# V tiles of a decode-attention kernel loaded on a second DMA queue

## The chip, the cores and the metric

The kernel runs on one core of a Trainium2 chip. The metric is the device time of one execution in microseconds, the median of several runs. The engines are TensorE (PE), VectorE (DVE), ScalarE (ACT), GpSimd (POOL) and SyncE (SP). Loads from HBM to the on-chip memory are done by the core's 16 DMA engines; an engine's instruction queue issues them, and each issuing engine has a DMA queue of its own (SyncE's is q1 in the profile).

## What is computed

One decode step (one token for each of 4 batches) of a transformer block: attention over the last 4096 positions of a cache, then a gated MLP. Cut to what matters:

```python
# x [4,1,576]; k_cache, v_cache [4, 16, 16384, 128]; 32 query heads on 16 KV heads; all bf16
W = 4096
q = (layernorm(x) @ wq)                       # 32 heads of 128
k = k_cache[:, :, Sk - W:, :]                 # 64 MiB are read of it
v = v_cache[:, :, Sk - W:, :]                 # and 64 MiB of it
p = softmax(q . k * 128**-0.5)
h = x + (p @ v) @ wo
hn = layernorm(h)
out = h + (relu(hn @ W_gate) * (hn @ W_up)) @ W_down     # F = 4608
```

## The kernel before

The cache windows are cut into 16 K tiles and 16 V tiles of 4 MiB. Tile g holds four KV heads of batch g // 4, as 128 partitions of 32 KiB. Four slots of the on-chip array `arena` take them in turn (`ring_slot`, `NSLOT = 4`). W_q uses one of the slots first. From K4 and V0 on the order is K4, V0, K5, V1, and so on to K15, V11, then V12 to V15; from K6 and V2 on, K tiles alternate between slots 0 and 2 and V tiles between slots 1 and 3.

The program is written as one list of operations for each engine, with named dependencies (`Prog`). Each engine takes its list in order and waits by semaphore for what an operation depends on. `place` (L216) adds a load: it finds in `owner` who reads the 64-element blocks that it will overwrite, makes the load depend on that reader (`("QK", g)` or `("PV", g)`), and puts it on SyncE's list. `add_kv` (L235) does that for a K or V tile; its load is issued at L242. All loads but that of x (L337, ScalarE's queue) are on SyncE's list, in the order: W_q (L251, L255), the tiles, W_o (L266), the weights of the MLP (L269 to L278), W_down in five parts (L284).

What uses the tiles, for each g from 0 to 15:

- VectorE transposes K tile g in place (`turn_k`, L424), in one instruction or, for g = 4, 8 and 12, in two halves.
- TensorE then does QK g (`pe_qk`, L448 and the helper line L34): 32 matmuls. When it ends, the slot of K tile g is free.
- At the end of a batch (g = 3, 7, 11, 15) comes the softmax: row maximum, exponential, transpose (`soft`, L453 to L470), and `remap` (L475 on TensorE, L482 on ScalarE and L487 on VectorE), which lays out the probabilities for PV. For batch 0 it stands between the two halves of the transpose of K tile 4.
- From g = 4 on TensorE does PV g - 4 after QK g (`pe_pv`, L509 and L34): 32 matmuls that read V tile g - 4. When it ends, that slot is free.
- `select_o` (L519 to L526, on ScalarE and VectorE) takes the result of PV out of PSUM.

After QK15 follow, on TensorE's list: PV11, `remap` of the last batch, PV12 to PV15, the output projection (L617), the second layernorm, the gate and up projections (GU, L666), and W_down's (L690), which reads HHT, the hidden values transposed by VectorE at L679. GpSimd's list holds only memsets and selects that set up constants (L289 to L331).

Of the kernel before, what the change touches and what calls it, by code (L numbers as in the profile page):

```python
# [20 lines left out]
NTILE = B * KVH // 4  # L21
# [4 lines left out]
TILE = 16384  # L26
# [94 lines left out]
def bass_sequential_preLN__sliding_block_cached__glu_gated_reglu__decode_kernel(  # L121
# [12 lines left out]
    with ExitStack() as es:  # L134
        cnt = [0]

        def sb(name, shape, dt):
            return es.enter_context(nc.sbuf_tensor("sb_" + name, shape, dt))

        P = Prog()  # L140
# [8 lines left out]
        arena = sb("arena", [128, AW], BF16)  # L149
# [63 lines left out]
        land = {}  # L213
        uses = {}

        def place(name, off, size, reader, make, key=None):  # L216
            deps = []
            for blk in range(off // 64, (off + size) // 64):
                r = owner.get(blk)
                if r is not None and r not in deps:  # L220
                    deps.append(r)
                owner[blk] = reader
            semk = key or "d_" + "_".join(str(v) for v in name)
            P.dma("sync", ("L",) + name, make, semk, deps)
            land[name] = off

        ring = [(-1 - 2 * NTILE) % NSLOT]
# [1 line left out]
        def ring_slot():  # L229
            s = ring[0] % NSLOT  # L230
            ring[0] += 1
            return s


        def add_kv(kind, g):  # L235
            b, qd = divmod(g, 4)
            s = ring_slot()
            off = slot0 + s * TILE
            cache = A_k_cache if kind == "K" else A_v_cache
            src = cache[b, 4 * qd:4 * qd + 4, SK - WIN:SK, :].rearrange("a (p t) d -> p a (t d)", p=32)  # L240
            place((kind, g), off, TILE, ("QK", g) if kind == "K" else ("PV", g),
                  lambda e: e.dma_start(out=arena[:, off:off + TILE], in_=src), key=f"slot{s}")  # L242


        def main_rows(W):
# [2 lines left out]
        def last_rows(W):  # L248
# [3 lines left out]
        s = ring_slot()  # L252
        wq_off = slot0 + s * TILE
        place(("wq", 0), wq_off, TILE, "QMM",
              lambda e: e.dma_start(out=arena[:, wq_off:wq_off + TILE], in_=main_rows(A_wq)), key=f"slot{s}")  # L255
        for g in range(NTILE):
            add_kv("K", g)
            if g >= 4:
                add_kv("V", g - 4)
# [3 lines left out]
        for g in range(NTILE - 4, NTILE):  # L263
            add_kv("V", g)
        place(("wo",), WO_OFF, H * D, "WO",
              lambda e: e.dma_start(out=arena[:, WO_OFF:WO_OFF + H * D], in_=A_wo.rearrange("(p r) n -> p (r n)", p=128)))  # L266
        gu_off = {}
        off = WO_OFF + H * D
        place(("gu", 0, 4), off, F, ("GU", 1, 4), lambda e, off=off: e.dma_start(  # L269
            out=bass.AP(tensor=arena, offset=off, ap=[[2 * AW, 64], [1, F]]), in_=B_W_gate[512:576, :]))  # L270
        P.dma("sync", ("L", "gu", 1, 4), lambda e, off=off: e.dma_start(
            out=bass.AP(tensor=arena, offset=AW + off, ap=[[2 * AW, 64], [1, F]]), in_=B_W_up[512:576, :]), "d_gu_1_4")
# [9 lines left out]
        for r0, r1 in zip(WD_ROWS, WD_ROWS[1:]):  # L282
            place(("wd", r0), wd_off + r0 * D, (r1 - r0) * D, ("DOWN", 1),
                  lambda e, r0=r0, r1=r1: e.dma_start(  # L284
                      out=arena[:, wd_off + r0 * D:wd_off + r1 * D],
                      in_=B_W_down.rearrange("(p r) n -> p (r n)", p=128)[:, r0 * D:r1 * D]))
# [18 lines left out]
                                                in_=c_qm[:, :, :].rearrange("p q (h j) -> p q h j", j=4),  # L305
# [4 lines left out]
                                                in_=to_v[:, :, :].rearrange("p n (k a) -> p n k a", a=4),  # L310
# [14 lines left out]
        for sg in range(2):  # L325
            pool(f"c_toq{sg + 1}", lambda e, sg=sg: e.affine_select(
                out=toq[:, :, :, :], in_=toq[:, :, :, :],
                pattern=[[0, 16], [32 * (1 - 2 * sg), 4], [0, 2]], compare_op=ALU.is_ge, fill=0.0, base=31 * (1 - sg), channel_multiplier=2 * sg - 1),
                [f"c_toq{sg}"])
        pool("c_oT", lambda e: e.memset(oT[:, :, :], 0.0))  # L330
        pool("c_hnT", lambda e: e.memset(hnT[:, :, :], 0.0))  # L331
        dve("c_m4", lambda e: e.tensor_reduce(out=m4[:, :], in_=c_m4[:, :, :], axis=AX.X, op=ALU.max), ["c_m41"])
        dve("c_par0", lambda e: e.tensor_tensor(out=par[:, 0:1], in0=m4[:, 0:1], in1=m4[:, 2:3], op=ALU.add), ["c_m4"])
        dve("c_par", lambda e: e.tensor_scalar(out=par[:, 1:2], in0=par[:, 0:1], scalar1=-1.0, scalar2=1.0,
# [206 lines left out]
        def finish_o():  # L541
            for q in range(4):
                for qd in range(4):
# [17 lines left out]
                                              in_=bass.AP(tensor=e8, offset=0, ap=[[8, 128], [0, 4], [1, 8]])), ["c_e8", "c_selc0"])  # L561
# [47 lines left out]
        for a in range(8):  # L609
            for n in range(2):  # L610
                for j in range(4):
# [4 lines left out]
                    else:  # L616
# [6 lines left out]
                                             in_=bass.AP(tensor=psb, offset=512 + 224, ap=[[4096, 128], [1, 64], [0, 2]])), ["part1"])  # L623
# [27 lines left out]
        for g in range(2):  # L651
            for c in (4, 0, 1, 2, 3):
                part_ = c if c == 4 or (c == 3 and g) else 0
                for m in range(3):
                    for j in range(4):
                        first = m == 0 and j == 0 and (c in (0, 4) or part_ == 3)
                        deps = [("L", "gu", g, part_)] if first else []
# [20 lines left out]
        for i in range(2):  # L678
            dve(("HHT", i), lambda e, i=i: e.transpose(  # L679
                out=hhT[:, 576 * i:576 * i + 576].rearrange("p (r q) -> p r q", q=32),  # L680
                in_=bass.AP(tensor=pp, offset=3712 + 18 * i, ap=[[PPW, 128], [1, 18], [36, 32]])), [("HH", m) for m in range(3)])
# [14 lines left out]
        for r in range(36):  # L696
# [3 lines left out]
            for n in range(2):  # L700
                deps = []
# [39 lines left out]
```

## Time and profile before

| | |
|---|---|
| median of 3 runs | 378.30 us (378.28 to 378.32) |
| the profiled execution | 378.22 us |
| its span in the profile | 377.0 us |
| busy: TensorE, VectorE, ScalarE, GpSimd | 213.8, 228.8, 53.7, 10.5 us |
| bytes moved, mean rate | 159.74 MB, 424 GB/s |
| SyncE's queue: share of the 16 DMA engines' span | 98.7% |
| issue to landing, median: K tiles, V tiles | 26.3, 28.5 us |
| mean granted clock of TensorE | 0.796 of full speed |

Busy time is the time in which an engine executes. The share of a DMA queue is the time that its packets took, over 16 times the span. "Issue to landing" is the time from the DMA instruction to the arrival of its last byte, so it contains the wait behind earlier transfers. The lines of the chain "that ended last" follow back, from the last instruction, what released each step.

### The profile page before, as it was taken

To read this page: it belongs to the slowest core of one execution; us is meant where nothing else is said; L and a number is where in the kernel's file an instruction comes from. 1 tells how busy PE (TensorE), PEld (TensorE's weight loads), DVE (VectorE), ACT (ScalarE), POOL (GpSimd) and SP (SyncE) were. 2 spreads that over 40 slices of the span, in tenths; PEclk is the share of its full clock that TensorE was granted. 3 is DMA by queue.
4 is the path that set the end of the run, shared out by engine and by line. 5 is a ranking of instruction groups with operands and counts; after the bars stand their busy time and mean duration, and the time that the engine had idled before them with its cause. 6 is when DMAs were issued, how large, how long until landed. Compare 5 with 4: busy or idle time off the path is not lost.

```text
span 377.0 us, 2556 instructions
## 1 busy us (share of the span) xinstructions
PE 213.8 (57%) x1462; PEld 39.9 (11%) x694; DVE 228.8 (61%) x164; ACT 53.7 (14%) x84; POOL 10.5 (3%) x29
## 2 busy tenths in 40 slices
PE   0404443239919091749282844664655787886658
PEld 0000000001001010001010100110000101002316
DVE  4088878779292969584847778665749433333240
ACT  3093000211000114010101140101010411112010
POOL 8200000000000000000000000000000000000000
PEclk9966666659969788696877786989695968998686
DMA  8999999999999999999999999999999999999996
GB/s 334 445 445 428 405 445 442 396 442 445 398 435 445 442 433 403 442 445 435 407 436 445 435 414 431 441 438 431 417 442 438 426 417 442 418 433 437 427 414 256
DMA packets 6378, 159.74 MB, mean 424 GB/s; under 512 B 728, under 2 KB 864, under 8 KB 1248
## 3 DMA queue, kind: packets, MB, share of 16 engines
q1 hardware_dynamic: 6360, 159.59, 98.7%
q8 instruction: 8, 0.13, 0.1%
q14 instruction: 2, 0.02, 0.0%
q10 hardware_dynamic: 8, 0.00, 0.0%
HBM read 159.58 MB, written 0.00 MB: 423 GB/s over the span
## 4 chain that ended last, share of the span: by engine, by line
DMA 60%; PE 20%; DVE 18%; SPq 1%; issue 0%; ACT 0%
DMA sb_arena<-in_A_k_cache_dram 53%; DVE sb_arena L424 16%; PE psb L34 11%; DMA sb_arena<-in_B_W_down_dram 7%; PE psb L448 4%; PE psb L509 3%; PE psb L690 2%; DVE sb_o_tmp L522 1%; DVE sb_pp L487 1%; SPq L242 0%; PE psb L475 0%; SPq L255 0%; ACT sb_out_sb L709 0%; SPq L251 0%; DVE sb_f L534 0%
## 5 line engine op out<-in xcount | busy, mean ns | idle before, releaser
L424 DVE STREAM_TRANSPOSE sb_arena<-sb_arena 128x8192 f32<-128x8192 f32 (+1 forms) x19 | 139.9, 7366 | 67.3 <-DMA sb_arena<-in_A_k_cache_dram 67.3
L448 PE MATMUL psb<-sb_arena 128*32 128x512 bf16 x256 | 42.8, 633 | 119.6 <-DVE sb_arena L424 119.5
L34 PE MATMUL psb<-sb_arena,sb_pp 128*128 128x512 bf16 (+1 forms) x386 | 108.7, 392 | 0.0
L509 PE MATMUL psb<-sb_arena,sb_pp 128*128 128x512 bf16 x128 | 50.8, 397 | 8.9 <-DVE sb_o_tmp L522 8.9
L519 ACT COPY sb_o_tmp<-psb 32x512 f32<-32x512 f32 x32 | 18.5, 577 | 182.0 <-PE psb L34 181.7
L34 PE MATMUL psb<-sb_arena 128*32 128x512 bf16 x256 | 43.6, 642 | 0.0
L522 DVE TENSOR_TENSOR sb_o_tmp<-psb,sb_fm 32x512 f32<-32x512 f32 x32 | 21.7, 678 | 18.6 <-PE psb L34 18.1
L448 PEld LDWEIGHTS psb<-sb_arena 128*32 128x32 bf16 x256 | 9.5, 119 | 161.9 <-DVE sb_arena L424 132.7
L509 PEld LDWEIGHTS psb<-sb_arena,sb_pp 128*128 128x128 bf16 x128 | 12.8, 100 | 116.6 <-issue 116.6
L526 DVE TENSOR_REDUCE sb_o_sel<-sb_o_tmp 128x128 f32<-128x512 f32 x16 | 17.7, 1106 | 0.5
L467 ACT ACTIVATE sb_pp<-psb,sb_hx 128x1024 bf16<-128x1024 f32 x4 | 4.5, 1113 | 79.4 <-DVE sb_hx L464 79.4
L487 DVE TENSOR_TENSOR sb_pp<-psb,sb_m 128x1024 bf16<-128x1024 f32 x8 | 9.3, 1206 | 4.9 <-PE psb L475 4.9
L482 ACT ACTIVATE sb_pp<-psb,sb_m 128x512 bf16<-128x512 f32 x16 | 9.7, 690 | 14.9 <-PE psb L475 14.9
L525 DVE TENSOR_TENSOR sb_o_tmp<-sb_o_tmp,sb_fm 64x512 f32<-64x512 f32 x16 | 11.0, 689 | 0.5
L415 ACT COPY sb_arena<-sb_q_keep 32x256 bf16<-32x256 bf16 x8 | 9.7, 1451 | 0.1
L690 PE MATMUL psb<-sb_arena,sb_pp 128*32 128x272 bf16 (+1 forms) x70 | 7.6, 396 | 3.7 <-DMA sb_arena<-in_B_W_down_dram 3.7
L401 DVE CAST sb_pp<-psb 128x512 bf16<-128x512 f32 x1 | 2.4, 2427 | 10.5 <-PE psb L381 10.5
L470 DVE STREAM_TRANSPOSE sb_pp<-sb_pp 128x1024 bf16<-128x1024 bf16 x4 | 5.0, 1245 | 5.1 <-ACT sb_pp L467 5.1
L475 PE MATMUL psb<-sb_pp,sb_to_v 128*32 128x256 bf16 x64 | 4.3, 400 | 6.3 <-DVE sb_pp L470 6.3
L690 PEld LDWEIGHTS psb<-sb_arena,sb_pp 128*32 128x32 bf16 x70 | 6.0, 131 | 5.1 <-DMA sb_arena<-in_B_W_down_dram 3.9
L34 PE MATMUL psb<-sb_arena,sb_hnT 128*32 128x384 bf16 x80 | 6.5, 407 | 0.0
L381 PE MATMUL psb<-sb_arena,sb_xnT 128*32 128x512 bf16 x16 | 2.6, 628 | 6.3 <-DMA sb_arena<-in_A_wq_dram 6.3
(120 smaller groups left out, 81.5 us busy)
## 6 DMA issues: line engine op xcount, KB each, us to landing
sb_arena<-in_A_k_cache_dram SPq DMA_DIRECT2D x16, 4096.0 KB, 26.3
sb_arena<-in_A_v_cache_dram SPq DMA_DIRECT2D x16, 4096.0 KB, 28.5
sb_arena<-in_A_wo_dram SPq DMA_DIRECT2D x1, 4608.0 KB, 24.8
sb_arena<-in_B_W_gate_dram SPq DMA_DIRECT2D x1, 4608.0 KB, 27.7
sb_arena<-in_A_wq_dram SPq DMA_DIRECT2D x1, 4096.0 KB, 12.7
sb_arena<-in_B_W_up_dram SPq DMA_DIRECT2D x1, 3456.0 KB, 27.3
sb_arena<-in_B_W_down_dram SPq DMA_DIRECT2D x1, 2160.0 KB, 26.5
sb_arena<-in_B_W_down_dram SPq DMA_DIRECT2D x1, 1440.0 KB, 29.6
```

Source lines behind the costliest of these rows:

```text
L34: return e.add_instruction(mybir.InstMatmult(name=e.bass.get_next_instruction_name(), engine=mybir.EngineType.PE, ins=[e.lower_ap(rhs), e. ...
L415: act("QW", lambda e, i=i, q=q: e.copy(out=bass.AP(tensor=arena, offset=32 * i * AW + 2 * i + q, ap=[[AW, 32], [512, 16], [136, 4], [32, 4]]),
L424: dve(("TRA", g), lambda e: e.transpose(out=dst, in_=src), [("L", "K", g)] if lo == 0 else [])
L448: fn = lambda e, out_=out_, lhsT=lhsT, rhs=rhs, start=start, stop=stop: e.matmul(out_, lhsT=lhsT, rhs=rhs, start=start, stop=stop, skip_gr ...
L482: act(("EV", b, 0), lambda e, a=a: e.activation(out=bass.AP(tensor=pp, offset=2 * a, ap=[[PPW, 128], [8, 2], [32, 128], [1, 2]]), in_=bank ...
L487: dve(("EV", b, 1), lambda e, n=n: e.tensor_tensor(out=bass.AP(tensor=pp, offset=16 + 8 * n, ap=[[PPW, 128], [32, 128], [2, 4], [1, 2]]), ...
L509: fn = lambda e, lhsT=lhsT, rhs=rhs, k=k, j=j: e.matmul(bank[2 + j], lhsT=lhsT, rhs=rhs, start=(k == 0), stop=(k == 7), skip_group_check=True)
L519: act(("OSC", g), lambda e, j=j: e.copy(out=o_tmp[32 * j:32 * j + 32, 0:512], in_=bank[2 + j][32 * j:32 * j + 32, :]), [("PV", g), ("OSEL" ...
L522: dve(("OSD", g), lambda e, j=j: e.tensor_tensor(out=ot(32 * j, 32), in0=bank[2 + j][32 * j:32 * j + 32, :].rearrange("p (t d) -> p t d", ...
L525: dve(("OS", g), lambda e: e.tensor_tensor(out=ot(64, 64), in0=ot(64, 64), in1=fmb(64, 64), op=ALU.mult), [("OSC", g)])
L526: dve(("OSEL", g), lambda e: e.tensor_reduce(out=o_sel[:, qd, b, :], in_=o_tmp[:, 0:512].rearrange("p (t d) -> p d t", d=DH), axis=AX.X, o ...
L690: return lambda e: e.matmul(out_, lhsT=lhsT, rhs=w[:, lo:hi], start=start, stop=stop, skip_group_check=True)
```

## The change

`place` takes the issuing engine as an argument. For V tiles 0 to 11 the load goes on GpSimd's list instead of SyncE's; these loads are collected in `side` and appended after GpSimd's last memset. Their dependencies, slots and destinations are the same as before. Each of them has a semaphore of its own instead of its slot's. K tiles, V tiles 12 to 15 and all weights stay on SyncE's list, in the same order.

```diff
-        def place(name, off, size, reader, make, key=None):
+        def place(name, off, size, reader, make, key=None, eng="sync"):
...
             semk = key or "d_" + "_".join(str(v) for v in name)
-            P.dma("sync", ("L",) + name, make, semk, deps)
+            if eng == "sync":
+                P.dma(eng, ("L",) + name, make, semk, deps)
+            else:
+                side.append(lambda: P.dma(eng, ("L",) + name, make, semk, deps))
             land[name] = off
...
+        side = []
...
             place((kind, g), off, TILE, ("QK", g) if kind == "K" else ("PV", g),
-                  lambda e: e.dma_start(out=arena[:, off:off + TILE], in_=src), key=f"slot{s}")
+                  lambda e: e.dma_start(out=arena[:, off:off + TILE], in_=src), key=None if kind == "V" and g < NTILE - 4 else f"slot{s}",
+                  eng="gpsimd" if kind == "V" and g < NTILE - 4 else "sync")
...
         pool("c_hnT", lambda e: e.memset(hnT[:, :, :], 0.0))
+        for make in side:
+            make()
```

## The prediction

> **What bounds the kernel now.** I read the page's table of queues first, then the waits of SyncE's own queue and its timeline, then the landing of single transfers, and last the chain that ended last, from 252 us on.
>
> ```profile
> span 377.0 us, 2556 instructions
> q1 hardware_dynamic: 6360, 159.59, 98.7%
> L424 DVE STREAM_TRANSPOSE sb_arena<-sb_arena 128x8192 f32<-128x8192 f32 (+1 forms) x19 | 139.9, 7366 | 67.3 <-DMA sb_arena<-in_A_k_cache_dram 67.3
> ```
>
> One queue, SyncE's, moves 159.59 MB and keeps the 16 DMA engines 98.7% busy. The transposes on VectorE (8.71 us a K tile) wait 67.3 us in all for K. The timeline gives the pace: the transposes of K6 and K15 start on landing, at 103.20 and 278.16 us, so a pair of 4 MiB tiles takes 174.96 / 9 = 19.44 us: 9.72 us a tile, 431.5 GB/s.
>
> ```profile
> 46.13 0.54 SPq L242 DMA_DIRECT2D sb_arena<-in_A_v_cache_dram  x1
> 55.87 0.54 SPq L242 DMA_DIRECT2D sb_arena<-in_A_k_cache_dram  x1
> 66.97 0.53 SPq L242 DMA_DIRECT2D sb_arena<-in_A_v_cache_dram  x1
> 85.00 0.54 SPq L242 DMA_DIRECT2D sb_arena<-in_A_k_cache_dram  x1
> 92.01 0.54 SPq L242 DMA_DIRECT2D sb_arena<-in_A_v_cache_dram  x1
> ```
>
> These are V0, K5, V1, K6 and V2, each issued when its slot came free (after QK1, QK2, QK3, QK4 and PV0). V0 and V1 landed 27.6 and 26.2 us after issue, at 73.7 and 93.2. K3, K4 and K5 landed at 54.30, 64.02 and 83.46 (starts of their transposes), in the order of issue. Here is the queue's thinnest place: at 85.00, when K6 is issued, only V1 is left ahead, for 8.2 us more.
>
> ```profile
> 252.02 26.12 DMA sb_arena<-in_A_k_cache_dram
> 278.16 8.72 DVE sb_arena L424
> 290.74 0.58 PE psb L509
> 340.90 26.55 DMA sb_arena<-in_B_W_down_dram
> 367.49 7.54 PE psb L690 x66
> ```
>
> K15 lands at 278.14, is transposed, QK15 ends and PV11 starts at 290.74. From there TensorE, VectorE and ScalarE run a serial tail (softmax of the last batch, PV12 to PV15, the projections). The chain switches to W_down's transfer at 340.90, but the tail is almost as late: the first half of HHT is ready at about 365.6, 1.9 us before W_down's first part at 367.45; the last GU matmuls also waited some 0.4 us for W_up. So two paths end within 2.3 us of each other: all the bytes, and "PV11 starts, then the tail".
>
> **What the change moves.** No byte, no compute instruction and no slot. V0 to V11 leave SyncE's queue (12 issues of 0.54 us, none on the path) for GpSimd's, behind the last memset there, which ends at 12.2 us. Nothing is queued behind them on GpSimd, so their waits hold up nobody else; each has a semaphore of its own, which costs nothing that a row shows. Each tile still waits for the reader of its slot. K5, K6 and the rest no longer stand behind a V issue, but in the timeline they never did: each left as soon as its own QK ended. So the unblocking is worth 0.
>
> What does change is the order of delivery, if GpSimd's V tile shares the engines with K tiles issued before it. The trace of before has no two bulk queues at once. Its nearest row is x, issued on ScalarE's queue at 0.93 us, after W_q's 512 KB on SyncE's at 0.80; x was in use at 3.16 while the 512 KB landed at 4.0: another queue does not wait for the backlog. Ends for V's share are therefore nothing until K's queue is empty, and everything; I take half, since both tiles come in the same 128 rows of 32 KiB. In the Trainium skill, "DMA: Bandwidth & Descriptors", section "Queues, rings and completion order", says that each DMA engine serves its queues in turn, packet by packet; x's row agrees, and no run shows it for bulk.
>
> A transfer's fixed part: 512 KB took 3.2 us to land, 1.2 of it at 431.5 GB/s, so 2.0; I put 1.3 ahead of the data and 0.7 behind. An issue on GpSimd has no row; the ends are 0 and 3.5 us more than SyncE's (its longest row, the memset of L298), and I take 1.0, near its selects and larger memsets (0.95 for L330).
>
> Step 1: K4 loses its place. V0's data start beside K3's at about 47.4. K3's last 6.2 us take 12.4, landing at 60.5. V0 ends at 66.8. K4 ends when all three have, in V0's old place: 73.7 instead of 64.02, 9.7 later. QK3 ends at 60.5 + 8.7 + 3.9 = 73.1, and V1 is issued then; K5 and V1 share, and both are in by 93.2, where V1 was before.
>
> Step 2: the engines run dry. From K4's landing to QK4's end it is 85.0 - 64.0 = 21.0 us (half a transpose, the softmax of batch 0, the other half, QK4). QK4 now ends at 94.7, so K6 is issued at 94.7 and not at 85.0. The data of K5 and V1 are through at about 92.4; K6's start at 96.0. That is 3.6 us with nothing to move, where the queue was never empty. All bytes end 3.6 us later.
>
> Step 3: phase. PV0 runs 94.7 to 101.6, so V2's data start at 101.6 + 1.0 + 1.3 = 103.9, when K6 has 1.8 of its 9.7 us left. At half speed K6 ends at 107.5. K7, issued at 105.5 after QK5, follows until 126.9; V2 ends at 123.3. From there each queue has its next tile in time (K8 is issued near 121, V3 near 112.5), and both deliver one tile each 19.44 us. K15 ends at 126.9 + 8 x 19.44 = 282.4 and lands at 283.1 (before 278.14). V11 ends at 123.3 + 9 x 19.44 = 298.3 and lands at 299.0 (before 259.03 + 28.8 = 287.8). V11 is later by more than 3.6 because V12, on SyncE's queue behind K15, takes half the engines from 282.4 on, where before it came after V11.
>
> Step 4: the tail. QK15 would end at 283.1 + 8.7 + 3.9 = 295.7; V11 at 299.0 is last. PV11 starts 8.3 us later than 290.74, and the tail with it. The covers of 1.9 and 0.4 us are used up: 8.3 - 2.3 = 6.0. The bytes, 3.6 late, are now hidden behind it. The profiled execution took 378.22 us (span 377.0 and 1.2 around it; the median is 378.30): 378.22 + 6.0 = **384.2 us**.
>
> Bounds. With GpSimd's issue at 0, V2 lands 1.0 earlier and the sum is 383.2; at 3.5 it is about 386. The rate with both queues has the ends 423 GB/s (the page's mean over the span) and 444 (the answer for 24 to 44 us); over the 250 us from 46 to 298 that is +5.0 or -7.0 us. I keep 431.5, the row for the same tiles.
>
> **Rivals.**
>
> Uneven shares or another phase. All bytes up to K15 and V11 are through by 287.8 + 3.6 = 291.4, and V12 adds as much as V11 has left at K15's end. If both land together, QK15 ends at 291.4 + 12.6 = 304.0 and PV11 is 13.3 late: 389.2. If V11 is a whole tile behind, it lands at 301.1, 10.4 late: 386.3. The least is 7.0 late, when both waits end at once (382.9). With V starved outright, V12 to V14 could pass V11, three tiles or 29 us more: up to some 405. For this: nothing fixes the share. Against: equal rows. Chance 0.25 in all. The Trainium skill, "SBUF — State Buffer", section "SBUF: two separate sides" (its box on DMAs issued from GpSimd), speaks against the change: GpSimd cannot write its descriptors while VectorE holds their shared port in a two-port mode. The rows against its applying here: L424 does 8192 elements in 8.71 us, 0.94 a ns, and the other VectorE rows of the loop are no faster; if V's issues waited for L424 all the same, V would fall behind K, up to the 386.3 above.
>
> Nothing moves: V tiles are delivered in the order of issue after all, or V0's start is so late that K4 keeps its place. Then K6 leaves at 85.0 and everything stays: 378.3. For: 98.7% is already full. Against: x's row. Chance 0.08. The Trainium skill, "DMA: Bandwidth & Descriptors", section "Issuing engines are not separate DMA queues", says that the engine chosen only saves its issue time; taken alone that is this case, for 0.54 us an issue is off the path.
>
> Faster: two queues side by side move 444 GB/s instead of 431.5. From 46 to 298 us that takes back 7.0 of the tail's 8.3 and, with the covers, 6.0 - 7.0 = -1.0: 377.2. It decides from about 443 GB/s on. For: the answer for 24 to 44 us. Against: tile after tile, landings at 9.72 us over 175 us with the queue full. Chance 0.07.
>
> **How the numbers follow.** The forecast has 0.60 (382.9 to 386.3 with the cost of GpSimd's issue, 379 to 389 with the rate). A difference of 0.2%, 0.76 us, is about what a measurement of this kernel can tell. Faster: the third rival and a sliver of the forecast at the best rate, 0.08. Same: the second rival, 0.08. Slower: the rest, 0.84. The range goes from 378.0, which takes in "nothing moves", to 391.0, which takes in the tiles landing together with a slightly lower rate; left out are the faster case and a starved queue.
>
> **What would show it.** In the changed profile: 48 MiB on a queue of GpSimd's; K4's transpose starting near 73.7 instead of 64.02; K6 issued near 94.7 and a dip in the GB/s row just after 92 us, worth 3.6 us; K landings 19.44 us apart from K7 on; V11 landing near 299 and as what PV11 waits for; W_down no longer the last wait, with L690 waiting for VectorE's HHT. Wrong, if K4 lands at 64, if the pair's pace with both queues is far from 19.44 us, or if W_down's transfer still ends the chain.

## The result, and the profile after

The changed kernel takes 383.65 us (median of 4 runs, 383.32 to 384.02), the kernel before beside it 378.31 us: the ratio is 1.0141, 95% interval 1.0124 to 1.0159. It is 5.3 us slower. The profiled execution took 383.58 us (span 382.3).

Line numbers after differ from those before: V and K tiles are issued at L247, K's transpose is L432, PV is L517, HHT is L687, W_down's matmuls are L698, W_down is loaded at L290.

The page of the changed kernel, the DMA rows of its 40 slices (9.6 us each) and its queues (packets, MB, share of 16 engines):

```profile
DMA  8999999995999999999999999999999999999996
GB/s 330 439 439 439 434 401 425 439 439 223 384 437 439 440 435 434 415 425 425 439 439 437 435 432 418 425 428 435 439 439 432 427 425 422 456 417 447 400 421 259
q1 hardware_dynamic: 4632, 109.26, 66.8%
q0 software_dynamic: 1728, 50.33, 30.6%
```

q0 is GpSimd's queue, with the twelve V tiles. The tenth slice stands out: 223 GB/s and half busy, where the kernel before had no such slice. The stretch from 89 to 100 us, before and then after. The columns are the stretch, its length, the busy time of TensorE, of its weight loads, of VectorE, ScalarE and GpSimd (in brackets the number of instructions), TensorE's granted clock, the DMA share and GB/s:

```profile
89.00:100.00 11.00, 10.86 (x66) 1.80 (x26) 6.68 (x7) 1.16 (x2) 0.00 (x0) 1.00 1.00 427
```

```profile
89.00:100.00 11.00, 9.11 (x57) 1.42 (x23) 9.81 (x2) 0.00 (x0) 0.00 (x0) 0.80 0.58 232
```

The packet records of the trace place the gap: 15 of the 16 DMA engines end their last packet of K5 and V1 at 91.3 to 91.7 us (one straggler at 92.72), and the first packets of K6 start at 96.22 to 97.0 us. K6's issue, with K7's in the same row (before, K6 was issued at 85.00):

```profile
94.90 11.39 SPq L247 DMA_DIRECT2D sb_arena<-in_A_k_cache_dram  x2
```

The chain that ended last, changed kernel (start, us, what):

```profile
36.49 37.29 DMA sb_arena<-in_A_k_cache_dram
73.81 4.45 DVE sb_arena L432
...
105.75 23.40 DMA sb_arena<-in_A_k_cache_dram
129.18 8.72 DVE sb_arena L432
...
263.31 26.17 DMA sb_arena<-in_A_k_cache_dram
289.51 8.72 DVE sb_arena L432
...
302.14 0.32 PE psb L517
...
351.75 26.94 DMA sb_arena<-in_B_W_down_dram
378.74 1.63 PE psb L698 x20
```

The first line is K4: 37.29 us from issue to landing, at 73.79 instead of 64.00. Its transpose, the softmax of batch 0 and QK4 follow, and K6 is issued at 94.90 instead of 85.00. K15 lands at 289.49 (before 278.14), PV11 starts at 302.14 (before 290.74), and the end is again a part of W_down. All landings of W_down are 5.4 us later than before: its first part at 372.85 (367.45), its last at 380.12 (374.72).

Summed from the packets, the bytes moved fall behind those of the kernel before by 2.30 MB up to 105 us, 5.3 us at 431.5 GB/s, and are 2.29 MB behind at 340 us: all of it is lost in that one gap, and nothing more in the 190 us with two queues that follow.

### The profile page after: what moved, and what is told of

It is laid out like the page before. It is cut to its first block, busy times and chain, and to the rows that moved or that the text cites. A ratio compares the mean times of both kernels' runs of the same rounds, so it can differ in the third digit from the quotient of the medians.

```text
span 382.3 us, 2556 instructions
## 1 busy us (share of the span) xinstructions
PE 213.4 (56%) x1462; PEld 38.2 (10%) x694; DVE 228.6 (60%) x164; ACT 53.7 (14%) x84; POOL 17.0 (4%) x41
## 4 chain that ended last, share of the span: by engine, by line
DMA 57%; PE 21%; DVE 20%; issue 0%; ACT 0%; SPq 0%
DMA sb_arena<-in_A_k_cache_dram 50%; DVE sb_arena L432 16%; PE psb L34 13%; DMA sb_arena<-in_B_W_down_dram 7%; PE psb L456 4%; PE psb L517 3%; DVE sb_o_tmp L530 1%; DVE sb_pp L495 1%; PE psb L483 1%; PE psb L698 0%; DVE sb_pp L478 0%; DVE sb_hx L461 0%; ACT sb_pp L475 0%; SPq L290 0%; SPq L261 0%
## 5 line engine op out<-in xcount | busy, mean ns | idle before, releaser
L432 DVE STREAM_TRANSPOSE sb_arena<-sb_arena 128x8192 f32<-128x8192 f32 (+1 forms) x19 | 139.9, 7366 | 74.2 <-DMA sb_arena<-in_A_k_cache_dram 74.2
L34 PE MATMUL psb<-sb_arena,sb_pp 128*128 128x512 bf16 (+1 forms) x386 | 111.0, 399 | 0.0
L517 PE MATMUL psb<-sb_arena,sb_pp 128*128 128x512 bf16 x128 | 51.8, 404 | 17.8 <-DVE sb_o_tmp L530 8.9
L517 PEld LDWEIGHTS psb<-sb_arena,sb_pp 128*128 128x128 bf16 x128 | 13.0, 101 | 128.4 <-issue 115.3
L247 POOL DMA_DIRECT2D sb_arena<-in_A_v_cache_dram x12 | 6.5, 542 | 252.8 <-PE psb L34 181.7
L698 PE MATMUL psb<-sb_arena,sb_pp 128*32 128x272 bf16 (+1 forms) x70 | 6.7, 348 | 2.7 <-DMA sb_arena<-in_B_W_down_dram 2.7
L461 DVE TENSOR_REDUCE sb_hx<-psb 128x1 f32<-128x1024 f32 x4 | 4.9, 1224 | 1.9 <-PE psb L34 1.8
## 6 DMA issues: line engine op xcount, KB each, us to landing
sb_arena<-in_B_W_down_dram SPq DMA_DIRECT2D x1, 2160.0 KB, 21.9
```

The source lines that it names most:

```text
L34: return e.add_instruction(mybir.InstMatmult(name=e.bass.get_next_instruction_name(), engine=mybir.EngineType.PE, ins=[e.lower_ap(rhs), e. ...
L432: dve(("TRA", g), lambda e: e.transpose(out=dst, in_=src), [("L", "K", g)] if lo == 0 else [])
L517: fn = lambda e, lhsT=lhsT, rhs=rhs, k=k, j=j: e.matmul(bank[2 + j], lhsT=lhsT, rhs=rhs, start=(k == 0), stop=(k == 7), skip_group_check=True)
```

## Experiments

Two theories beside the prediction's: the queue itself costs (GpSimd's, or any second queue), or the tail ends the run, because K and V are out of step.

**Which tiles cost: V2 to V11 alone, and V0 alone.**

```diff
-                  ... key=None if kind == "V" and g < NTILE - 4 else f"slot{s}",
-                  eng="gpsimd" if kind == "V" and g < NTILE - 4 else "sync")
+                  ... key=None if kind == "V" and 2 <= g < NTILE - 4 else f"slot{s}",      # V2 to V11
+                  eng="gpsimd" if kind == "V" and 2 <= g < NTILE - 4 else "sync")
+                  # and, in the other kernel, g == 0 in both places: V0 alone
```

> V0 and V1 stay on SyncE's queue, V2 to V11 go on GpSimd's. Theory 'dry spell' (V0 beside K3 and K4 delays K4 by 9.8 us, so K6 is issued 9.9 us late and the DMA engines have nothing for 5 us): K4 lands near 64.0, K6 is issued near 85, no dry spell, the last part of W_down lands at 374.7 as before; time 378.3 to 379.5, the excess if the tail shows. Rival 'the queue costs' (GpSimd's queue, or two queues at once, cost by the tile, 5.3 / 12 = 0.44 us each): 10 tiles, 382.7. Rival 'tail' (K and V land out of step, PV11 starts late and the serial tail ends the run): PV11 still 6 us late or more, 382 to 384.

> Only V0 goes on GpSimd's queue, all other tiles on SyncE's in their old order. 'Dry spell': K4 near 73.8, K6 issued near 95, 5 us with nothing to move, last W_down near 380; time 383.3 to 383.9, the whole loss from one tile of twelve. 'The queue costs': one tile, 378.3 + 0.44 = 378.7. 'Tail': K15 and V11 are in step again and 5 us late, less the cover of 2.3: near 381.

V2 to V11: 379.3 us (378.02 to 382.1, 10 runs), ratio 1.0040 (1.0013 to 1.0066). V0 alone: 383.5 us (383.34 to 383.78), ratio 1.0145 (1.0130 to 1.0160), as slow as the full change. The stretch from 89 to 100 us, V2 to V11 and then V0 alone:

```profile
89.00:100.00 11.00, 10.53 (x65) 1.79 (x26) 6.85 (x7) 1.16 (x2) 0.69 (x1) 1.00 0.99 427
```

```profile
89.00:100.00 11.00, 8.89 (x55) 1.31 (x23) 10.52 (x2) 0.00 (x0) 0.00 (x0) 0.78 0.57 235
```

With ten tiles on GpSimd's queue K4 lands at 64.14, K6 is issued at 85.08, and the last W_down lands at 375.01. With V0 alone there, the numbers are 73.86, 94.95 and 380.16. So the bytes of these ten tiles come at most 0.3 us late on the second queue (375.01 against 374.72), and V0's place costs all 5.3 us. V1 was not moved by itself. "The queue costs" by the tile falls.

V2 to V11 still loses 1 us in the median and scatters over 4. In its profile TensorE's wait ahead of W_down's matmuls is for VectorE:

```profile
PE psb L698 <- DVE sb_pp L687: 2.0, 1, 2.0
```

That is the tail. The bytes are in time, but K15 lands at 284.50 (before 278.14), because K and V share where K used to come first, and the tail starts 6.4 us later. The five fastest of the ten runs, 378.0 to 379.0 us, have a mean granted clock of 0.80 or more; of the five others, 379.6 to 382.1 us, four are below 0.80, and one with 0.815 took 380.05. That fits a tail bound by TensorE, but was not tested by itself, and two kernels below with the same kind of tail do not bear it out: with V0 held until K4 had landed, 378.86 and 379.40 us had 0.788 and 380.76 us had 0.816, and with the softmax first 379.29 us had 0.792 and 381.68 us had 0.803. These are means over the whole span; what makes the tail scatter stays open.

**Another second queue.** V0 to V11 on ScalarE's queue, each issue put where ScalarE's next operation waits for the same PV.

```diff
-                side.append(lambda: P.dma(eng, ("L",) + name, make, semk, deps))
+                side.append(lambda: P.dma("scalar", ("L",) + name, make, semk, deps))
...
-        for make in side:
-            make()
...
         put_q()
+        for g in range(2):
+            side[g]()
...
             pe_pv(g)
+            if g + 2 < NTILE - 4:
+                side[g + 2]()
```

> V0 to V11 on ScalarE's queue instead of GpSimd's; each issue stands in ScalarE's list where what follows it waits for the same PV anyway. 'Dry spell': as with GpSimd, K4 near 73.7, a gap of 4 to 5 us, 383 to 384. 'The queue costs', in the form that GpSimd's is the dear one: near 378.3.

383.81 us (383.44 to 384.03), ratio 1.0151 (1.0134 to 1.0168). K4 lands at 73.80, K6 is issued at 94.86, the last W_down lands at 380.26. The loss does not depend on which of these two engines issues.

**V0 held back.** All twelve tiles on GpSimd's queue, but V0 also waits for K4 to land, or for K3.

```diff
             semk = key or "d_" + "_".join(str(v) for v in name)
+            if name == ("V", 0):
+                deps.append(("L", "K", 4))          # or ("L", "K", 3)
```

> As the changed kernel, all twelve on GpSimd's queue, but V0's issue also waits until K4 has landed. 'Dry spell': K4 near 64.0, K6 issued near 85, no gap, last W_down near 374.7; 378.3 to 379.5. 'The queue costs': twelve tiles, 383.6. 'Tail': PV11 still several us late, 381 to 384.

> As the changed kernel, but V0's issue also waits until K3 has landed (54.3 us): half a dose. 'Dry spell': K3 lands at 54.3, V0 then shares with K4, which lands near 72; K6 is issued near 93 instead of 94.9, the gap is 5.0 - 1.9 = 3 us, and all bytes are 3.3 late: last W_down near 378, time 381 to 382.5 with the tail. 'The queue costs': 383.6, no smaller than with the full change. If a late K4 were not the cause, the gap would not follow K6's issue.

Waiting for K4: 380.8 us (378.86 to 382.14, 6 runs), ratio 1.0070 (1.0043 to 1.0097). K4 lands at 64.07, K6 is issued at 85.01, there is no gap, and the last W_down lands at 374.70, as before: the bytes have lost nothing. What is left, some 2.7 us, is again the tail (K15 at 285.29; L700, W_down's matmuls in this kernel, does not wait for W_down). The time was above my 379.5; there I had underrated the tail.

Waiting for K3: 380.06 us (379.3 to 380.09), ratio 1.0057 (1.0042 to 1.0072). Here I was wrong about the dose. V0 was issued at 54.73, but its first packet came at 59.09, when about 70% of K4's data had moved, and K4 landed at 68.68, not 72. K6 left at 89.68, and the gap was small: in the stretch from 89 to 100 us the engines moved 381 GB/s, against 427 before.

```profile
89.00:100.00 11.00, 10.73 (x69) 1.79 (x26) 10.82 (x7) 1.15 (x2) 0.53 (x1) 0.97 0.93 381
```

The last W_down landed at 375.83, 1.1 us late. K6's issue at 85.0, 89.7 and 94.9 goes with 0, 1.1 and 5.4 us lost, so the slack ends shortly before 89.7. That agrees roughly with the packets of the changed kernel: K6's first come 1.3 to 2.1 us after its issue, and most engines run out at about 91.5.

**The softmax first.** The order of transfers stays as changed; only VectorE's list differs, so that QK4 ends sooner after K4's landing.

```diff
-                turn_k(g, 0, 1)
                 if g == 4:
                     soft(0)
+                turn_k(g, 0, 1)
```

> The changed kernel with batch 0's softmax ahead of the first half of K4's transpose on VectorE: it then runs while K4 is still coming. Order of transfers as in the changed kernel, K4 near 73.8. 'Dry spell': from K4's landing to QK4's end 17 us instead of 21, K6 issued near 90.7, the gap 1 us instead of 5, last W_down near 376; time 379 to 381 with the tail. 'The queue costs': 383.6, as nothing about the queues differs.

379.29 us (378.83 to 381.68, 9 runs), ratio 1.0056 (1.0036 to 1.0075). K4 still lands late, at 73.67, but K6 is issued at 90.16; the last W_down lands at 375.44.

```profile
89.00:100.00 11.00, 8.10 (x45) 1.16 (x10) 8.09 (x1) 1.15 (x2) 0.53 (x1) 0.96 0.93 387
```

With the same queues and the same late K4, 4.7 of the 5.4 us of late bytes are gone, once K6 no longer has to wait so long for QK4. That closes the chain V0, K4, QK4, K6, gap.

**What ends the changed kernel: a longer tail, more bytes.**

```diff
+        for i in range(2):                        # longer tail, ahead of L654
+            dve(None, lambda e, i=i: e.tensor_reduce(out=o_sel[:, i, 0, :], in_=o_tmp[:, 0:512].rearrange("p (t d) -> p d t", d=DH),
+                                                axis=AX.X, op=ALU.add), [("OSEL", NTILE - 1), "OT"])
```

```diff
+        spare = sb("spare", [128, 4096], BF16)    # more bytes, ahead of W_down
+        P.dma("sync", ("L", "spare"), lambda e: e.dma_start(out=spare[:, :], in_=main_rows(B_W_gate)[:, 0:4096]), "d_spare")
```

> The changed kernel with two more reductions of 1.03 us each on VectorE ahead of L654, in the serial tail after PV15; nothing else moves. If the bytes end the changed kernel: the last W_down still lands near 380.1, and the tail's 2.1 us are covered for the most part by L698's waits for W_down (0.1 + 1.1 + 0.7 us): 383.6 to 384.3. If the tail ends it: 385.7.

> The changed kernel with one load of 1 MiB more on SyncE's queue, ahead of W_down's five parts, into memory that nothing reads: 1.05 MB / 431.5 GB/s = 2.43 us of bytes. If the bytes end the changed kernel: last W_down near 382.5, time 386.0. If the tail ends it: 383.6 to 384.3.

Both raise the time: the longer tail to 386.38 us (385.5 to 387.16), the extra bytes to 386.31 us (385.88 to 387.25), each 2.7 us above the changed kernel's 383.65 (3.3 us, when each is taken against the kernel before that was measured beside it, 377.71 here and 378.31 there). I had expected the first to be covered, and it wasn't. In the profile of the longer tail the matmuls of W_down (L701) wait for HHT alone, and in that of more bytes (L700) for W_down, whose last part lands at 382.71:

```profile
PE psb L701 <- DVE sb_pp L690: 2.0, 1, 2.0
```

```profile
PE psb L700 <- DMA sb_arena<-in_B_W_down_dram: 2.6, 2, 2.0
```

So the two paths of the changed kernel end close together, and lengthening either is paid. In its profile the bytes come last: W_down's matmuls end at 380.37, 0.25 us after its last part landed. Where these matmuls waited for HHT alone they ended 6.4 us after they went on (370.53 to 376.90 with V2 to V11, 377.08 to 383.45 with the longer tail); from 372.94 in the changed kernel that would be 379.3, so the tail had about 1 us to spare in that execution (an estimate from these rows). On ScalarE's queue HHT came at 374.69, 2 us later than here, and W_down's bytes still came last (380.26, the matmuls' end 380.51). How much of the 2.7 is the added rows is left open: they took 1.94 us, and in this execution the tail ran at a granted clock of 0.88, against 0.93 in the changed kernel's.

None of these kernels beats the one before: there the bytes flow without a gap and K15 lands earliest, and every variant loses one or the other.

## Why the prediction was right, and where it was not

384.2 us was forecast and 383.65 measured. The cause, V0 ahead of K4 and the dry spell that follows, is the one forecast. The path from there to the time is not: steps 2 to 4 were mis-sized, the run ends on W_down's bytes and not on the tail, and that the sum comes out within 0.6 us is luck.

- **Step 1 (K4 loses its place) held.** K4 landed at 73.79 (73.7 forecast), V1 at 93.20 (93.2), K5 at 92.00; V0 landed at 70.14, later than the 67.5 meant, because its first packet came 4.8 us after its issue (46.44 to 51.20). Step 1 had put 1.3 there (46.13 to 47.4), and left out the 1.0 for an issue on GpSimd that step 3 counts. K3, slowed for less long, landed at 58.00 (60.5). Half shares held too. Queues of the changed kernel from 130 to 160 us (packets, MB, share):

```profile
q0 software_dynamic: 215, 6.52, 50.6%
q1 hardware_dynamic: 207, 6.26, 48.4%
```

  The Trainium skill, "DMA: Bandwidth & Descriptors", section "Queues, rings and completion order", has each engine take its queues in turn, packet by packet; these near-equal counts agree with it (199 and 191 of the packets are of 32 KiB).

- **Step 2 (the dry spell) held in kind, and its size was too small.** K6 left at 94.90 (94.7). The gap was forecast as 3.6 us and cost 5.3 in bytes. The mis-sized term is where the data ended: I put that at 92.4 from V1's landing, but a landing is that of the slowest engine, and 15 of the 16 had run out at about 91.5. At the other end K6's first packets came 1.3 us after its issue, as I had it, but on some engines not before 97.0. On average over the 16 engines the data ended at 91.57 and went on at 96.61.

- **Step 3 (phase): V right, K wrong.** V11 landed at 298.04 (299.0). K15 landed at 289.49 (283.1), and PV11 waited for QK15 instead, so that it started 11.4 us late (8.3). I had each queue supplied in time; but K10 was issued at 167.69, when 15 of the 16 engines had moved their last of K9, and its first packet came at 171.93. In between V5 had the engines to itself: it landed 15.9 us after V4, and K10 21.9 us after K9. From K7 to K15 a tile took (289.49 - 129.15) / 8 = 20.0 us, not 19.44; all of the excess is in K8 to K11 (20.3, 19.9, 21.9 and 20.6 us), and from K12 on each took 19.4. For K8, K9 and K11 the cause stays open. With V0 alone moved PV11 started only some 5.4 us late (QK15 ended near 296.3), so the other 6 are the price of sharing; in the time they are hidden behind W_down's bytes (383.5 us with V0 alone, 383.65 with all twelve).

- **Step 4 (the tail) had two errors that cancelled.** The tail began later than forecast, but from PV11 to the first half of HHT it took 70.6 us instead of 74.8, so HHT came 7.2 us later and not 11.4. Mean granted clock in the two stretches (last columns: clock, DMA share, GB/s), before and then after:

```profile
290.74:365.55 74.81, 57.05 (x416) 11.69 (x182) 26.67 (x49) 13.04 (x24) 0.00 (x0) 0.86 1.00 427
```

```profile
302.14:372.73 70.59, 52.94 (x415) 10.84 (x182) 26.68 (x49) 13.03 (x24) 0.00 (x0) 0.93 1.00 428
```

  VectorE and ScalarE are busy for the same time, TensorE for 4.1 us less, at the higher granted clock. Why the clock was higher is not shown. With PV11's delay as measured and the tail of before, the sum would have been 378.22 + 11.4 - 2.3 = 387.3 us. I said that W_down would no longer be the last wait, and named it as a sign of being wrong if its transfer still ended the chain. It did:

```profile
PE psb L698 <- DMA sb_arena<-in_B_W_down_dram: 2.7, 2, 2.0
```

  W_down's first part (372.85) and HHT (372.73) arrive within 0.2 us of each other. What sets the time is that W_down's bytes come 5.4 us late; the run is 5.3 us longer, here as with V0 alone.

- **The rivals.** "Nothing moves" fell with K4's landing. "Faster" fell on the rate: 431 GB/s from 100 to 282 us with both queues, as with one. The phase lay between the one that I picked, with V11 15.9 us behind K15, and the rival in which both land together: V11 landed 8.6 us behind K15. GpSimd blocked by VectorE did not show: V0's issue took 0.69 us at 46.44, in the middle of K2's transpose, and the others 0.53. The box of the Trainium skill, "SBUF — State Buffer", section "SBUF: two separate sides", which speaks of VectorE's two-port modes, so had no bearing on these rows:

```profile
46.44 0.69 POOL L247 DMA_DIRECT2D sb_arena<-in_A_v_cache_dram  x1 [34.24 <-PE psb L34]
70.97 0.53 POOL L247 DMA_DIRECT2D sb_arena<-in_A_v_cache_dram  x1 [23.84 <-PE psb L34]
```

  V0's first packet, at 51.20, also came before that transpose ended (43.22 + 8.71 = 51.93), and V1's and V2's came as long after their issue (4.4 and 4.3 us). On ScalarE's queue this took 3.8 us for each of the three, and on SyncE's 4.2 us for K10, so GpSimd's extra is at most the 1.0 that I gave it; what was wrong is the 1.3 us ahead of the data for a tile beside a busy queue.

## What to carry to other kernels

Where one queue already kept the DMA engines busy, a second queue added no bytes a second (431 GB/s either way); it changed who came first. A transfer that is moved to another queue can take up to half of the engines' time from all that was issued before it, as it did here with packets of one size, so ask which of those is needed first, and what will be issued when it has been used: one V tile, issued 39 us ahead of its use, cost 1.4% here. Where two paths end within a couple of microseconds, price both; a sum along one of them can be right by luck.

## What the runs showed of the hardware

Packets of 32 KiB took a median of 1.21 us on either queue, in turn or alone, and a DMA issued from GpSimd 0.53 us, as from SyncE. A 4 MiB transfer had its first packet 1.3 us after its issue on idle engines, but on an empty queue beside a busy one 3.8 us (ScalarE's), 4.2 us (SyncE's, K10) and 4.3 to 4.8 us (GpSimd's) after it, which fits engines that first finish what they had taken from the busy queue (not tested). Its landing came 0.4 to 0.5 us after its last packet of data with one queue busy, and up to about 1.7 us with two. The same instructions of the tail took 70.6 to 74.8 us from one profiled execution to another, with granted clocks of 0.93 and 0.86 to 0.88; the clock is not all of it, for at 0.88 it took 71.7 us in one kernel and 74.7 in another.
